# Two-scale attention and a gated FFN: attention on small array tiles, with x kept transposed on the chip

## The chip, the core and the metric

The kernel runs on one core of a Trainium2 chip. A core has five engines with instruction streams of their own: PE (TensorE, matmuls and weight loads), DVE (VectorE), ACT (ScalarE), POOL (GpSimd) and SP (SyncE, which here only issues transfers). Matmuls read SBUF and write PSUM. Sixteen DMA engines move data between DRAM and SBUF. The metric is the device time of one execution in microseconds (us), the median of several runs.

## The reference

```python
def _attn_ref(q, k, v):                       # each 8 x 8 x 576 x 64, float32
    factor = 4; Sd = S // factor; scale = 1.0 / np.sqrt(D)
    def sm_attn(qq, kk, vv):
        s = scale * np.matmul(qq, kk.transpose(0, 1, 3, 2))
        s = s - np.max(s, axis=-1, keepdims=True)
        a = np.exp(s)
        a = a / (np.sum(a, axis=-1, keepdims=True) + 1e-09)
        return np.matmul(a, vv)
    q_d = q.reshape(B, H, Sd, factor, D).mean(axis=3)      # k_d, v_d likewise
    out_up = np.repeat(sm_attn(q_d, k_d, v_d), factor, axis=2)
    mask = np.abs(pos[:, None] - pos[None, :]) < factor    # 7 keys for each query
    scores = np.where(mask, scale * np.matmul(q, k.transpose(0, 1, 3, 2)), -1e9)
    ...                                                    # softmax of the band
    return out_up + np.matmul(attn, v)

def _moe_ref(x, w_gate, w_val, w_out):        # x: 4608 tokens x 512
    gate = np.maximum(x @ w_gate, 0.0)        # 512 x 1536
    return gate * (x @ w_val) @ w_out         # 1536 x 512
```

x is the attention's output with the eight heads side by side. So each head has a coarse attention (144 x 144, over means of four rows), repeated four times, and a local one in which a query sees seven keys.

## The kernel before

**Pairs and chunks.** The 64 heads are taken as 32 pairs (hp); a pair's two heads lie on partitions 0-63 and 64-127 of the transposed tiles. The FFN takes 512 tokens at a time: nine chunks, each of 12 h tasks and 4 y tasks. An h task is 8 matmuls of 512 columns (4 for the gate at L170, 4 for the value at L175), a relu on ACT (L180) and a product on DVE (L182). A y task is 12 matmuls of 512 columns (L191) and a copy (L195). All matmul operands are float16.

**Loads.** `emit_load` issues q and k (L261) and two windows of v (L292) for a pair on SP's queue, 96 or 128 partitions with pieces of 64 floats, two pairs ahead. Weights come on ACT's queue as float32 (L140) and are cast there (L145).

**Attention of a pair.** `emit_mid` casts q on ACT (L301, L302), k and v on DVE (L303, L304, L307). `emit_mid_b` turns q and k on PE with an identity (L319, 12 matmuls), copies them out (L328 ACT, L330 DVE) and sums groups of four rows on DVE (L336, L342). `emit_compute` makes the coarse scores (L366), means of v (L377), the local scores in blocks of 96 queries by 128 keys (L405), exponentials without a maximum subtracted (L389, L415), a multiplication by a 0/1 band (L418), coarse output (L429), local output with a column of ones for the sum (L463), the coarse output repeated by a matmul (L475), and the normalised sum into `x_b` (L486, L492).

**x.** `x_b` goes to DRAM (L503) and comes back turned by transposing DMAs (L153), 512 tokens by 128 features at a time.

**Order.** The tile framework keeps the program's order on each engine and adds the waits. Two lists per pair (`sched`) put FFN tasks between its parts, 16 tasks over four pairs, the first in the second half of pair 5; tasks that don't fit run after the last pair (`tail`). Attention and FFN share eight PSUM buffers of one bank.

Of the kernel before, what the change touches and what calls it, by code (L numbers as in the profile page):

```python
# [14 lines left out]
DEBUG_MODE = "full"  # L15


def _np_constants():
    i = np.arange(128)[:, None]
    p = np.arange(96)[None, :]  # L20
    band = ((i - p >= 0) & (i - p <= 6)).astype(np.float16)
    m_first = band * (i >= 3)
    m_last = band * (i <= 98)
    masks = np.stack([m_first, band, band, band, band, m_last], axis=1)
    P72 = np.zeros((128, 3, 72), np.float16)
    rw = np.arange(3, 99)
    for sig in range(3):
        P72[rw, sig, 24 * sig + (rw - 3) // 4] = 0.25
    E72 = np.zeros((128, 3, 96), np.float16)
    t = np.arange(72)  # L30
    qq = np.arange(96)
    for a in range(3):
        E72[:72, a, :] = t[:, None] == (24 * a + qq[None, :] // 4)
    I96 = np.zeros((96, 128), np.float16)
    I96[:, :96] = np.eye(96)
    return masks, P72, E72, I96
# [17 lines left out]
def kernel(  # L54
# [12 lines left out]
    NH = B * H  # L67
    NP = NH // 2
    NQ = 96
    NB = S // NQ  # L70
    SD = S // 4
    KPAD = 16
    KW = KPAD + S + 32
    scale = float(1.0 / np.sqrt(D))
    D_MODEL = H * D
    D_FF = moe_w_gate.shape[1]
# [3 lines left out]
    NJJ = D_FF // 128  # L80

    masks_np, P72_np, E72_np, I96_np = _np_constants()
    masks_dr = nc.inline_tensor(masks_np, name="band_masks").ap()
    P72_dr = nc.inline_tensor(P72_np, name="p72").ap()
    E72_dr = nc.inline_tensor(E72_np, name="e_up").ap()
    I96_dr = nc.inline_tensor(I96_np, name="i96").ap()

    cpool = ctx.enter_context(tc.tile_pool(name="consts", bufs=1))
    masks_sb = cpool.tile([128, 6, 96], FP16, name="masks_sb")
    P72_sb = cpool.tile([128, 3, 72], FP16, name="p72_sb")  # L90
    E_sb = cpool.tile([128, 3, 96], FP16, name="E_sb")
    I96_sb = cpool.tile([96, 128], FP16, name="I96_sb")
    nc.sync.dma_start(masks_sb, masks_dr)
    nc.sync.dma_start(P72_sb, P72_dr)
    nc.sync.dma_start(E_sb, E72_dr)
    nc.sync.dma_start(I96_sb, I96_dr)

    drpool = ctx.enter_context(tc.tile_pool(name="scratch", bufs=1, space=bass.MemoryType.DRAM))
    x_dr = drpool.tile([NTOK, D_MODEL], FP16, name="x_dr")
    probe_dr = nc.dram_tensor("probe", (3, 128, KW), mybir.dt.float16, kind="Internal").ap() if DEBUG_MODE == "probe" else None  # L100

    wpool = ctx.enter_context(tc.tile_pool(name="weights", bufs=1))
    wg_sb = wpool.tile([128, 4, D_FF], FP16, name="wg_sb")
    wv_sb = wpool.tile([128, 4, D_FF], FP16, name="wv_sb")
    wo_sb = wpool.tile([128, NJJ, D_MODEL], FP16, name="wo_sb")
    wstg = ctx.enter_context(tc.tile_pool(name="wstage", bufs=5))

    psum = ctx.enter_context(tc.tile_pool(name="psum", bufs=8, space=bass.MemoryType.PSUM))
    a_nat = ctx.enter_context(tc.tile_pool(name="a_nat", bufs=8))
    a_vst = ctx.enter_context(tc.tile_pool(name="a_vst", bufs=4))  # L110
    a_16 = ctx.enter_context(tc.tile_pool(name="a_16", bufs=3))
    a_T = ctx.enter_context(tc.tile_pool(name="a_T", bufs=4))
    a_dT = ctx.enter_context(tc.tile_pool(name="a_dT", bufs=4))
    a_vw = ctx.enter_context(tc.tile_pool(name="a_vw", bufs=4))
    a_e = ctx.enter_context(tc.tile_pool(name="a_e", bufs=8))
# [3 lines left out]
    a_sm = ctx.enter_context(tc.tile_pool(name="a_sm", bufs=8))
    a_t2 = ctx.enter_context(tc.tile_pool(name="a_t2", bufs=4))  # L120
    a_x = ctx.enter_context(tc.tile_pool(name="a_x", bufs=2))
    f_xT = ctx.enter_context(tc.tile_pool(name="f_xT", bufs=8))
    f_r = ctx.enter_context(tc.tile_pool(name="f_r", bufs=3))
    f_gT = ctx.enter_context(tc.tile_pool(name="f_gT", bufs=20))
    f_y = ctx.enter_context(tc.tile_pool(name="f_y", bufs=1))

    wtasks = []
    for kk in range(4):
        wtasks.append((moe_w_gate, kk, wg_sb, kk))
        wtasks.append((moe_w_val, kk, wv_sb, kk))  # L130
    for jj in range(NJJ):
        wtasks.append((moe_w_out, jj, wo_sb, jj))

    st_w = {}

    def emit_wdma(i):
        src, row, dst, slot = wtasks[i]
        ncol = src.shape[1]
        t = wstg.tile([128, ncol], FP32, name="wstage", tag="wstage")
        nc.scalar.dma_start(t, src[bass.ts(row, 128), :])  # L140
        st_w[i] = t

    def emit_wcast(i):
        src, row, dst, slot = wtasks[i]
        nc.scalar.copy(out=dst[:, slot, :], in_=st_w.pop(i))  # L145

    ffn_state = {}

    def ffn_xbar1(c, m):
        if c not in ffn_state:  # L150
            ffn_state[c] = {"xT": [None] * 4, "gts": [], "y_sb": None}
        t = f_xT.tile([128, TCH], FP16, name="xT", tag="xT")
        nc.sync.dma_start(  # L153
            out=t,
            in_=_dap(x_dr, c * TCH * D_MODEL + m * 128, [[D_MODEL, TCH], [1, 128]]),
            transpose=True,
        )
        ffn_state[c]["xT"][m] = t

    def ffn_xbars(c):  # L160
        for m in range(4):
            ffn_xbar1(c, m)

    def ffn_task_h(c, jj):
        st = ffn_state[c]
        xts = st["xT"]
        h1 = psum.tile([128, TCH], FP32, name="h1_ps", tag="bank")
        h2 = psum.tile([128, TCH], FP32, name="h2_ps", tag="bank")
        for kk in range(4):
            nc.tensor.matmul(  # L170
                out=h1, lhsT=wg_sb[:, kk, bass.ts(jj, 128)], rhs=xts[kk],
                start=(kk == 0), stop=(kk == 3),
            )
        for kk in range(4):
            nc.tensor.matmul(  # L175
                out=h2, lhsT=wv_sb[:, kk, bass.ts(jj, 128)], rhs=xts[kk],
                start=(kk == 0), stop=(kk == 3),
            )
        r1 = f_r.tile([128, TCH], FP16, name="r1", tag="r1")
        nc.scalar.activation(out=r1, in_=h1, func=AF.Relu)  # L180
        gt = f_gT.tile([128, TCH], FP16, name="gT", tag="gT")
        nc.vector.tensor_tensor(out=gt, in0=r1, in1=h2, op=ALU.mult)  # L182
        st["gts"].append(gt)

    def ffn_task_y(c, ty):
        st = ffn_state[c]
        if st["y_sb"] is None:
            st["y_sb"] = f_y.tile([128, 4, D_MODEL], FP32, name="y_sb", tag="y_sb")
        y_ps = psum.tile([128, D_MODEL], FP32, name="y_ps", tag="bank")
        for jj in range(NJJ):  # L190
            nc.tensor.matmul(  # L191
                out=y_ps, lhsT=st["gts"][jj][:, bass.ts(ty, 128)],
                rhs=wo_sb[:, jj, :], start=(jj == 0), stop=(jj == NJJ - 1),
            )
        nc.scalar.copy(out=st["y_sb"][:, ty, :], in_=y_ps)  # L195
        if c == NCH - 1:
            nc.scalar.dma_start(
                _dap(out, (c * TCH + ty * 128) * D_MODEL,
                     [[D_MODEL, 128], [1, D_MODEL]]),
                st["y_sb"][:, ty, :],  # L200
            )
            if ty == 3:
                ffn_state.pop(c)
        elif ty == 3:
            nc.scalar.dma_start(
                _dap(out, c * TCH * D_MODEL,
                     [[D_MODEL, 128], [128 * D_MODEL, 4], [1, D_MODEL]]),
                st["y_sb"],
            )
            ffn_state.pop(c)  # L210

    def emit_task(t):
        kind = t[0]
        if kind == "h":
            ffn_task_h(t[1], t[2])
        elif kind == "y":
            ffn_task_y(t[1], t[2])
        elif kind == "wd":
            emit_wdma(t[1])
        elif kind == "wc":  # L220
            emit_wcast(t[1])

# [292 lines left out]
    for i in pre_dmas:  # L515
        emit_wdma(i)
# [50 lines left out]
```

## Time and profile before

| | us |
|---|---|
| median of 3 runs | 441.1 (439.14 to 441.73) |
| span of the profiled execution | 440.1 |
| busy in it: PE, DVE, ACT, POOL | 397.4, 298.4, 211.4, 7.7 |
| first FFN matmul starts | 71.8 |
| last copy of y starts | 436.4 |

The span is the time from the first to the last instruction of one execution; what lies around it is not in the profile. A row of the profile's groups reads: line, engine, operation, out<-in, count, busy time, mean of one. "PEld" are weight loads, which overlap matmuls. A matmul's record contains its latency (0.2 us), so records of consecutive matmuls overlap, and their price is the distance of their starts. "SPq" is an instruction that issues a transfer: its time is that of the issue, not of the data.

The rows that the change replaces, from the groups of instructions by shape:

```profile
L415 ACT ACTIVATE e_sb<-sc_ps 128x288 f16<-128x288 f32 x128 | 42.0, 416 | 1.1 <-PE sc_ps L405 1.1
L418 DVE TENSOR_TENSOR e_sb<-e_sb,masks_sb 128x288 f16<-128x288 f16 x128 | 36.3, 301 | 4.9 <-ACT e_sb L415 4.9
...
L475 PE MATMUL f_ps<-odn,E_sb 72*96 72x64 f16 x384 | 25.6, 220 | 0.0
...
L342 DVE TENSOR_REDUCE k_dT<-kT 128x144 f16<-128x576 f16 x32 | 23.7, 740 | 0.0
...
L389 ACT ACTIVATE e_d<-sd_ps 72x288 f16<-72x288 f32 x64 | 22.5, 402 | 16.9 <-PE sd_ps L366 16.8
...
L307 DVE CAST vwin<-vst 128x768 f16<-128x768 f32 x32 | 17.7, 553 | 6.5 <-DMA vst<-in_v_dram 6.5
```

### The profile page before, as it was taken

How to read it: one execution, taken by the hardware profiler on the slowest of the kernel's cores; microseconds unless marked ns; L12 is line 12 of the kernel's file. 1: busy time of each engine (PE TensorE's matmuls, PEld its weight loads, DVE VectorE, ACT ScalarE, POOL GpSimd, SP SyncE). 2: the span in 40 equal slices, each digit the busy share in tenths (PEclk: the TensorE clock that was granted, in tenths of full speed). 3: DMA queues.
4: the chain of work that ended last, by engine and by line, in shares of the span. 5: the costliest groups of instructions: out<-in, count | busy, mean ns of one | idle time of the engine just before them, and what ended most of it. 6: DMA issues, size and time to landing. Idle time of an engine off the chain costs nothing.

```text
span 440.1 us, 9037 instructions
## 1 busy us (share of the span) xinstructions
PE 397.4 (90%) x3408; PEld 227.6 (52%) x3408; DVE 298.4 (68%) x812; ACT 211.4 (48%) x485; POOL 7.7 (2%) x100
## 2 busy tenths in 40 slices
PE   0037778999999999999999999999999999999996
PEld 0026675555555555555565556555655654444442
DVE  0229998998789878977997799779966860330430
ACT  2435876564565455545564556445633532332331
POOL 0000000000000000000000000000000000000000
PEclk9999999999999999999999999999999999999999
DMA  8799989457777787577775646321123112200202
GB/s 288 245 311 224 278 226 243 107 114 174 188 185 172 166 207 176 135 165 215 173 162 132 191 105 138 76 105 33 30 36 109 27 39 48 97 0 9 87 0 95
DMA packets 171730, 60.64 MB, mean 138 GB/s; under 512 B 164264, under 2 KB 164520, under 8 KB 171688
## 3 DMA queue, kind: packets, MB, share of 16 engines
q1 hardware_dynamic: 164008, 41.21, 42.5%
q10 hardware_dynamic: 7680, 18.88, 11.4%
q8 instruction: 26, 0.43, 0.4%
q14 instruction: 16, 0.13, 0.1%
HBM read 41.20 MB, written 14.16 MB: 126 GB/s over the span
## 4 chain that ended last, share of the span: by engine, by line
PE 82%; DMA 7%; DVE 6%; SPq 3%; issue 1%; ACT 1%; DVEq 0%
PE h_ps L170 21%; PE h_ps L175 21%; PE y_ps L191 19%; PE tp_ps L319 3%; PE f_ps L475 3%; PE od_ps L429 3%; PE u_ps L463 3%; DMA vst<-in_v_dram 3%; PE vd_ps L377 3%; PE sc_ps L405 2%; DMA nat<-in_k_dram 2%; SPq L292 2%; PE sd_ps L366 1%; DMA out_dram<-y_sb 1%; DMA masks_sb<-band_masks 1%; SPq L261 1%
## 5 line engine op out<-in xcount | busy, mean ns | idle before, releaser
L170 PE MATMUL h_ps<-xT,wg_sb 128*128 128x512 f16 x432 | 112.1, 382 | 0.0
L175 PE MATMUL h_ps<-xT,wv_sb 128*128 128x512 f16 x432 | 111.7, 381 | 0.0
L191 PE MATMUL y_ps<-wo_sb,gT 128*128 128x512 f16 x432 | 95.7, 379 | 0.0
L175 PEld LDWEIGHTS <-wv_sb 128*128 128x128 f16 x432 | 42.5, 98 | 51.6 <-issue 1.1
L191 PEld LDWEIGHTS <-gT 128*128 128x128 f16 x432 | 41.5, 98 | 48.2
L170 PEld LDWEIGHTS <-wg_sb 128*128 128x128 f16 x432 | 40.3, 99 | 42.3 <-issue 1.6
L195 ACT COPY y_sb<-y_ps 128x512 f32<-128x512 f32 x36 | 21.1, 586 | 78.8 <-PE y_ps L191 72.8
L415 ACT ACTIVATE e_sb<-sc_ps 128x288 f16<-128x288 f32 x128 | 42.0, 416 | 1.1 <-PE sc_ps L405 1.1
L418 DVE TENSOR_TENSOR e_sb<-e_sb,masks_sb 128x288 f16<-128x288 f16 x128 | 36.3, 301 | 4.9 <-ACT e_sb L415 4.9
L463 PEld LDWEIGHTS <-e_sb 128*96 128x96 f16 x384 | 24.8, 138 | 12.0 <-DVE e_sb L418 6.5
L463 PE MATMUL u_ps<-vwin,e_sb 128*96 128x65 f16 x384 | 25.3, 220 | 6.2 <-DVE e_sb L418 6.2
L389 ACT ACTIVATE e_d<-sd_ps 72x288 f16<-72x288 f32 x64 | 22.5, 402 | 16.9 <-PE sd_ps L366 16.8
L394 DVE CAST vd_sb<-vd_ps 72x130 f16<-72x130 f32 x64 | 15.6, 284 | 20.4 <-PE vd_ps L377 20.4
L330 DVE CAST kT<-tp_ps 128x288 f16<-128x288 f32 x64 | 26.7, 442 | 1.5 <-PE tp_ps L319 1.5
L475 PE MATMUL f_ps<-odn,E_sb 72*96 72x64 f16 x384 | 25.6, 220 | 0.0
L429 PE MATMUL od_ps<-vd_sb,e_d 72*72 72x65 f16 x256 | 18.4, 206 | 7.8 <-DVE vd_sb L394 5.9
L328 ACT CAST qT<-tp_ps 128x288 f16<-128x288 f32 x64 | 23.5, 431 | 0.8 <-PE tp_ps L319 0.5
L342 DVE TENSOR_REDUCE k_dT<-kT 128x144 f16<-128x576 f16 x32 | 23.7, 740 | 0.0
L336 DVE TENSOR_REDUCE q_dT<-qT 128x144 f16<-128x576 f16 x32 | 23.6, 739 | 0.0
L475 PEld LDWEIGHTS <-E_sb 72*96 72x96 f16 x384 | 22.8, 138 | 0.0
L307 DVE CAST vwin<-vst 128x768 f16<-128x768 f32 x32 | 17.7, 553 | 6.5 <-DMA vst<-in_v_dram 6.5
L429 PEld LDWEIGHTS <-e_d 72*72 72x72 f16 x256 | 16.9, 123 | 10.0 <-issue 3.8
(556 smaller groups left out, 452.9 us busy)
## 6 DMA issues: line engine op xcount, KB each, us to landing
vst<-in_v_dram SPq DMA_DIRECT2D x62, 192.0 KB
nat<-in_q_dram SPq DMA_DIRECT2D x32, 288.0 KB
nat<-in_k_dram SPq DMA_DIRECT2D x32, 288.0 KB
out_dram<-y_sb ACTq DMA_DIRECT2D x8, 1024.0 KB
x_dr<-x_b SPq DMA_DIRECT2D x32, 144.0 KB
wstage<-in_moe_w_gate_dram ACTq DMA_DIRECT2D x4, 768.0 KB
wstage<-in_moe_w_val_dram ACTq DMA_DIRECT2D x4, 768.0 KB
wstage<-in_moe_w_out_dram ACTq DMA_DIRECT2D x12, 256.0 KB
```

The costliest lines, as they stand in the source:

```text
L170: nc.tensor.matmul(out=h1, lhsT=wg_sb[:, kk, bass.ts(jj, 128)], rhs=xts[kk], start=(kk == 0), stop=(kk == 3),)
L175: nc.tensor.matmul(out=h2, lhsT=wv_sb[:, kk, bass.ts(jj, 128)], rhs=xts[kk], start=(kk == 0), stop=(kk == 3),)
L191: nc.tensor.matmul(out=y_ps, lhsT=st["gts"][jj][:, bass.ts(ty, 128)], rhs=wo_sb[:, jj, :], start=(jj == 0), stop=(jj == NJJ - 1),)
L328: nc.scalar.copy(out=o, in_=tp)
L330: nc.vector.tensor_copy(out=o, in_=tp)
L336: nc.vector.tensor_reduce(out=q_dT, in_=qT[:, KPAD : KPAD + S].rearrange("p (t f) -> p t f", f=4), axis=mybir.AxisListType.X, op=ALU.add,)
L342: nc.vector.tensor_reduce(out=k_dT, in_=kT[:, KPAD : KPAD + S].rearrange("p (t f) -> p t f", f=4), axis=mybir.AxisListType.X, op=ALU.add,)
L415: nc.scalar.activation(out=esb, in_=scps[hh][:, :, 0:NQ], func=AF.Exp, scale=scale)
L418: nc.vector.tensor_tensor(out=esb, in0=esb, in1=masks_sb[:, 3 * g2 : 3 * g2 + 3, :], op=ALU.mult,)
L429: nc.tensor.matmul(out=od_ps[0:72, hh, tcx, :], lhsT=ed_sb[hh][:, c, bass.ts(tcx, 72)], rhs=vd_sb[hh][:, c, :], start=(c == 0), stop=(c == 1),
L463: nc.tensor.matmul(out=up[:, j, :], lhsT=e_sb[hh][j // 3][:, j % 3, :], rhs=vw[:, hh, j, :], start=True, stop=True,)
L475: nc.tensor.matmul(out=fp[:, j, :], lhsT=E_sb[0:72, j % 3, :], rhs=odn_sb[hh][0:72, j // 3, :], start=True, stop=True,)
```

## The change

Nearly the whole kernel is rewritten. What it does now:

- **x stays in SBUF, transposed** (`xT`, 128 x 4 x 4608 float16). `sums` makes the attention's output features by tokens, so the DRAM copy and its transposing DMAs are gone.
- **Local attention in blocks of 24 queries and 32 keys.** `scores` issues 48 matmuls of 64 x 32 by 32 columns on eight tiles of the array; `sums` 48 of 32 x 64 by 24 columns on eight tiles. The band is added as 0 or -1e9, and rows are normalised before `sums`.
- **Exact maxima** for both scales (`maxima`), subtracted before the exponentials: on POOL for the local rows (`dd`), as the bias of four ACT instructions for the coarse ones. Normalising is on POOL too (`weigh`); local weights are turned 32 by 32 on DVE (`turn_p`), coarse ones by a transposing DMA (`adT`).
- **q and k** are turned on PE for pairs 0 to 5 (`turn_pe`, which also sums groups of four by matmul), and by two transposing DMAs for the others (`turn_dma`, with the sums on POOL in `pool_qk`).
- **Weights** come by DMAs on POOL's queue that cast on the way; no cast on ACT.
- **One PSUM buffer `at` of four banks** for the attention, and four one-bank buffers for the FFN.
- **The order is written by hand.** Slots 0 to 3 carry no FFN work. In slot s the scores of pair s and the sums of pair s-1 stand between FFN units: 3, 3, 2, 2, 2 units in slots 4 to 8, four in the others (two before the sums, two after), and 36 units at the end.

```diff
-    x_dr = drpool.tile([NTOK, D_MODEL], FP16, name="x_dr")
-    psum = ctx.enter_context(tc.tile_pool(name="psum", bufs=8, space=bass.MemoryType.PSUM))
+    xT = pool.tile([128, 4, NTOK], FP16, name="xT")
+    fpsum = ctx.enter_context(tc.tile_pool(name="fps", bufs=4, space=bass.MemoryType.PSUM))
+    at = psum.tile([128, 4, 512], FP32, name="at")
...
+    def load_w(src, dst, lo, hi):
+        nc.gpsimd.dma_start(
+            dst[:, :, lo:hi], src.rearrange("(a p) f -> p a f", p=128)[:, :, lo:hi]
+        )
...
+    def turn_dma(p):
+        nc.sync.dma_start(
+            qT[p % 3][:, 0:S].rearrange("p (j t) -> p j t", j=6),
+            q16[p % 2].rearrange("p j f -> p (j f)"),
+            transpose=True,
+        )
...
+    def pool_qk(p):
+        qg = qT[p % 3][:, 0:S].rearrange("p (g f) -> p g f", f=4)
+        nc.gpsimd.tensor_tensor(out=ptq, in0=qg[:, :, 0:2], in1=qg[:, :, 2:4], op=ALU.add)
+        nc.gpsimd.tensor_tensor(
+            out=pd[p % 3][:, 0, :], in0=ptq[:, :, 0], in1=ptq[:, :, 1], op=ALU.add
+        )
...
+    def scores(p):
...
+                out=at[32 * x : 32 * x + 32, kc, 288:416],
+                lhsT=p32,
+                rhs=vt[:, :, m, :],
...
+                    out=at[0:72, h, 144 * c : 144 * c + 144],
+                    lhsT=pdt[lo : lo + 64, 0, 72 * c : 72 * c + 72],
+                    rhs=pdt[lo : lo + 64, 1, :],
...
+        for n in range(6):
+            for g in range(4):
+                c, m = n // 3, 4 * (n % 3) + g
+                for h in range(2):
+                    lo = 64 * h
+                    nc.tensor.matmul(
+                        out=at[32 * g : 32 * g + 32, 2 + h, 32 * n : 32 * n + 32],
+                        lhsT=qt[lo : lo + 64, 96 * n + 24 * g : 96 * n + 24 * g + 32],
+                        rhs=kt[lo : lo + 64, c, :, 6 * m : 6 * m + 8].rearrange("p r g -> p g r"),
+                        start=True,
+                        stop=True,
+                        tile_position=(lo, 32 * g),
+                    )
...
+    def maxima(p):
+        c = col[p % 2]
+        nc.vector.tensor_tensor(
+            out=sm[p % 2].rearrange("p (h n) j -> p h (n j)", h=2),
+            in0=at[:, 2:4, 0:192],
+            in1=_sap(mask, (0, 128), 0, [[0, 2], [1, 192]]),
+            op=ALU.add,
+        )
...
+        nc.vector.tensor_reduce(out=c[:, 0:12], in_=sm[p % 2], axis=AX.X, op=ALU.max)
+        nc.gpsimd.tensor_tensor(
+            out=dd[p % 2],
+            in0=sm[p % 2],
+            in1=_sap(c, (0, 128), 0, [[1, 12], [0, 32]]),
+            op=ALU.subtract,
+        )
...
+    def exps(p):
...
+        nc.scalar.activation(out=ee[p % 2], in_=dd[p % 2], func=AF.Exp, scale=scale)
+        nc.scalar.copy(out=vd16[p % 2], in_=at[:, 0:2, 288:416])
...
+    def weigh(p):
...
+        nc.gpsimd.tensor_tensor(
+            out=pp[p % 2],
+            in0=ee[p % 2],
+            in1=_sap(c, (0, 128), 24, [[1, 12], [0, 32]]),
+            op=ALU.mult,
+        )
...
+    def sums(p):
+        vt, w, vd, ad = vw[p % 4], pT[p % 2], vd16[p % 2], adT[p % 2]
+        for n in range(6):
+            for h in range(2):
+                for g in range(4):
                     nc.tensor.matmul(
+                        out=at[64 * h : 64 * h + 64, g, 24 * n : 24 * n + 24],
+                        lhsT=vt[32 * g : 32 * g + 32, h, n, :],
+                        rhs=w[32 * g : 32 * g + 32, 6 * h + n, 0:24],
...
+        nc.scalar.copy(
+            out=odx[p % 2].rearrange("p (g n m) -> p g n m", g=4, n=6),
...
+        nc.vector.tensor_tensor(
+            out=xT[:, kk, b * S : (b + 1) * S].rearrange(
...
+    for s in range(4, NP + 1):
+        a = per_slot.get(s, (1, 1, 1, 1))
...
+        if s + 3 < NP and s > 3:
+            load(s + 3)
+        if s < NP:
+            if s + 1 < NP and s + 1 >= N_PE:
+                pool_qk(s + 1)
+            if s + 2 < NP:
+                cast_q(s + 2, "act")
+            scores(s)
+            maxima(s)
+        ffn(a[0])
+        if s + 1 < N_PE:
+            turn_pe(s + 1)
+        if s < NP:
+            exps(s)
+            if s + 2 < NP:
+                cast_v(s + 2, "dve")
+            weigh(s)
+        ffn(a[1])
+        if s > 4:
+            sums(s - 1)
+        if s + 2 < NP:
+            cast_k(s + 2, 0, "act")
+            cast_k(s + 2, 1, "act")
+            turn_dma(s + 2)
+        ffn(a[2])
+        if s < NP:
+            turn_p(s)
+        ffn(a[3])
+    ffn(len(units) - pos[0])
```

More of the change, by code (lines that the diff above doesn't have):

```diff
@@ L14 @@
 ALU = mybir.AluOpType
-DEBUG_MODE = "full"
+AX = mybir.AxisListType
+N_PE = 6
+NEG = -1.0e9
 def _np_constants():
[L19 to L36, printed above, removed]
+    p = np.arange(128)
+    g, i = p // 32, p % 32
+    j = np.arange(32)
+    diff = (j[None, :] - 4) - i[:, None]
+    inside = np.abs(diff) <= 3
+    mask = np.zeros((128, 6, 32), np.float32)
+    for n in range(6):
+        key = 24 * (4 * n + g)[:, None] - 4 + j[None, :]
+        ok = inside & (key >= 0) & (key < 576)
+        mask[:, n, :] = np.where(ok, 0.0, NEG)
+    mask[i >= 24] = 0.0
+    p32 = np.zeros((128, 32), np.float16)
+    own = (i >= 4) & (i < 28)
+    p32[p[own], (6 * g + (i - 4) // 4)[own]] = 0.25
+    eye = np.zeros((96, 192), np.float16)
+    eye[:, :96] = np.eye(96)
+    eye[1:73, 96:168] = np.eye(72)
+    eye[np.arange(96), 168 + np.arange(96) // 4] = 1.0
+    return mask, p32, eye
 def _dap(t_ap: bass.AP, extra_off: int, dims) -> bass.AP:
@@ L119 @@
[L119 to L155, printed above, removed]
+    NJ = DF // 128
@@ new lines, in many @@
+    def many(n, shape, dt, name):
+        return [pool.tile(shape, dt, name=f"{name}{i}") for i in range(n)]
+    wg = pool.tile([128, 4, DF], FP16, name="wg")
+    wv = pool.tile([128, 4, DF], FP16, name="wv")
+    wo = pool.tile([128, NJ, DM], FP16, name="wo")
+    qst = many(3, [96, 2, 6, 64], FP32, "qst")
+    kst = many(3, [80, 2, 2, 256], FP32, "kst")
+    vst = many(3, [128, 2, 6, 64], FP32, "vst")
+    y_sb = many(4, [128, DM], FP32, "y_sb")
+    q16 = many(2, [96, 6, 128], FP16, "q16")
@@ L156, in ffn_xbar1 @@
+    def turn_dma(p):
+        nc.sync.dma_start(
+            qT[p % 3][:, 0:S].rearrange("p (j t) -> p j t", j=6),
+            q16[p % 2].rearrange("p j f -> p (j f)"),
             transpose=True,
         )
[L158 to L172, printed above, removed]
-            )
[L174 to L210, printed above, removed]
@@ L310, in emit_mid_b @@
[L310 to L318 removed]
+        nc.sync.dma_start(
+            kT[p % 3].rearrange("p c r g -> p (c r) g"),
+            k16[p % 2].rearrange("p c r f -> p (c r f)"),
+            transpose=True,
+        )
@@ new lines, in exps @@
+    def exps(p):
+        c = col[p % 2]
+        for h in range(2):
+            for cc in range(2):
+                hc = 2 * h + cc
+                nc.scalar.activation(
+                    out=e_d[p % 2][0:72, h, cc, 0:6, 0:24],
+                    in_=at[0:72, h, 144 * cc : 144 * cc + 144].rearrange("p (n j) -> p n j", j=24),
+                    func=AF.Exp,
+                    bias=c[0:72, 40 + hc : 41 + hc],
+                    scale=scale / 16.0,
+                    accum_out=c[0:72, 44 + hc : 45 + hc],
+                )
+        nc.scalar.activation(out=ee[p % 2], in_=dd[p % 2], func=AF.Exp, scale=scale)
+        nc.scalar.copy(out=vd16[p % 2], in_=at[:, 0:2, 288:416])
@@ L425, in emit_compute @@
-        od_ps = psum.tile([72, 2, 2, 65], FP32, name="od_ps", tag="bank")
-        for hh in (0, 1):
-            for tcx in range(2):
-                for c in range(2):
-                    nc.tensor.matmul(
-                        out=od_ps[0:72, hh, tcx, :],
-                        lhsT=ed_sb[hh][:, c, bass.ts(tcx, 72)],
-                        rhs=vd_sb[hh][:, c, :],
-                        start=(c == 0),
-                        stop=(c == 1),
-                    )
-        odn_sb = [None, None]
@@ new lines, with unit_h @@
+    n_h = [0]
+    n_y = [0]
+    def unit_h(c, j):
+        h1 = fpsum.tile([128, TCH], FP32, name="h1_ps", tag="f")
+        h2 = fpsum.tile([128, TCH], FP32, name="h2_ps", tag="f")
+        for ps, w in ((h1, wg), (h2, wv)):
+            for kk in range(4):
+                nc.tensor.matmul(
+                    out=ps,
+                    lhsT=w[:, kk, 128 * j : 128 * j + 128],
+                    rhs=xT[:, kk, TCH * c : TCH * c + TCH],
+                    start=(kk == 0),
+                    stop=(kk == 3),
+                )
+        r = r1[n_h[0] % 3]
+        n_h[0] += 1
+        nc.scalar.activation(out=r, in_=h1, func=AF.Relu)
+        nc.vector.tensor_tensor(out=gT[c % 2][:, j, :], in0=r, in1=h2, op=ALU.mult)
@@ new lines, in unit_y @@
+    def unit_y(c, t):
+        ps = fpsum.tile([128, DM], FP32, name="y_ps", tag="f")
+        for j in range(NJ):
+            nc.tensor.matmul(
+                out=ps,
+                lhsT=gT[c % 2][:, j, 128 * t : 128 * t + 128],
+                rhs=wo[:, j, :],
+                start=(j == 0),
+                stop=(j == NJ - 1),
+            )
+        y = y_sb[n_y[0] % 4]
+        n_y[0] += 1
+        nc.scalar.copy(out=y, in_=ps)
+        nc.sync.dma_start(
+            _dap(out, (c * TCH + t * 128) * DM, [[DM, 128], [1, DM]]), y
+        )
@@ new lines, with ffn @@
+    units = []
+    for c in range(NCH):
+        for j in range(NJ):
+            units.append(("h", c, j))
+            if c and j % 3 == 1:
+                units.append(("y", c - 1, j // 3))
+    units += [("y", NCH - 1, t) for t in range(4)]
+    pos = [0]
+    def ffn(n):
+        for _ in range(n):
+            kind, c, j = units[pos[0]]
+            pos[0] += 1
+            (unit_h if kind == "h" else unit_y)(c, j)
+    nc.sync.dma_start(eye, eye_dr)
+    for t in kst[0], vst[0]:
+        nc.gpsimd.memset(t, 0.0)
@@ new lines, with cast_early @@
+    load(0)
+    nc.scalar.dma_start(p32, p32_dr)
+    nc.scalar.dma_start(mask, mask_dr)
+    for t in k16 + e_d:
+        nc.vector.memset(t, 0.0)
+    load(1)
+    load(2)
+    for t in qT:
+        nc.gpsimd.memset(t[:, S:], 0.0)
+    def cast_early(p):
+        cast_q(p, "act")
+        cast_k(p, 0, "dve")
+        cast_k(p, 1, "dve")
+        cast_v(p, "pool")
+    cast_early(0)
+    turn_pe(0)
+    w_at = {1: [0], 2: [1], 3: [2, 3]}
+    for s in range(4):
+        cast_early(s + 1)
+        scores(s)
[3 more added lines that the diff above has]
+        weigh(s)
+        for i in w_at.get(s, ()):
+            load_w(moe_w_gate, wg, 384 * i, 384 * i + 384)
+            load_w(moe_w_val, wv, 384 * i, 384 * i + 384)
+        load(s + 3)
+        turn_p(s)
+        if s:
+            sums(s - 1)
@@ new lines @@
+    sums(3)
+    load_wo(0, 4)
+    load_wo(4, 8)
+    load_wo(8, 12)
+    per_slot = {4: (1, 1, 1, 0), 5: (1, 1, 1, 0), 6: (1, 1, 0, 0), 7: (1, 1, 0, 0), 8: (1, 1, 0, 0)}
+    for s in range(4, NP + 1):
+        a = per_slot.get(s, (1, 1, 1, 1))
+        if s == 4:
+            cast_q(5, "act")
+            cast_k(5, 0, "act")
+            cast_k(5, 1, "act")
+            cast_v(5, "dve")
+        if s + 3 < NP and s > 3:
+            load(s + 3)
+        if s < NP:
[3 more added lines that the diff above has]
+                cast_q(s + 2, "act")
+            scores(s)
+            maxima(s)
+        ffn(a[0])
+        if s + 1 < N_PE:
+            turn_pe(s + 1)
+        if s < NP:
+            exps(s)
+            if s + 2 < NP:
+                cast_v(s + 2, "dve")
+            weigh(s)
+        ffn(a[1])
+        if s > 4:
+            sums(s - 1)
+        if s + 2 < NP:
[4 more added lines that the diff above has]
+        if s < NP:
+            turn_p(s)
+        ffn(a[3])
```

514 lines of the change are left out of this document (193 added, 321 removed).

## The prediction

> **What bounds the kernel now.** I read the page's engine rows first, then its forty slices, then the chain that ended last.
>
> ```profile
> PE 397.4 (90%) x3408; PEld 227.6 (52%) x3408; DVE 298.4 (68%) x812; ACT 211.4 (48%) x485; POOL 7.7 (2%) x100
> ...
> PE   0037778999999999999999999999999999999996
> ...
> DMA  8799989457777787577775646321123112200202
> ...
> PE 82%; DMA 7%; DVE 6%; SPq 3%; issue 1%; ACT 1%; DVEq 0%
> ```
>
> There are two regimes. For six slices (66 us) PE is not full while the DMA engines are; then PE is full to the end. The windows of one stretch of each, 10 to 70 us and four pairs of the steady part (columns: length, busy time and instructions of PE, PEld, DVE, ACT, POOL, granted clock, DMA share, GB/s):
>
> ```profile
> 10.00:70.00 60.00, 32.50 (x386) 28.54 (x387) 41.07 (x128) 37.09 (x79) 1.07 (x15) 1.00 0.96 252
> ...
> 148.87:192.59 43.72, 43.65 (x409) 24.97 (x408) 36.82 (x103) 22.63 (x56) 1.22 (x15) 1.00 0.74 174
> ```
>
> In the steady part four pairs take 43.72 us, 10.93 each, and PE has no gap. The chain's y rows have 24 matmuls of 512 columns in 5.18 us, 0.2158 each (0.42 ns a column). Four pairs carry 144 such, 31.1 us; the remaining 12.6 are attention, 3.16 us of PE a pair. All 1296 FFN matmuls take 279.7 us. The first one starts at 71.97, the last matmul ends at 436.3, and copy, store and end take 3.8: 72 + 279.7 + 26.5 pairs x 3.16 + 3.8 = 439, against the span of 440.1. So the time is: start of the FFN, plus a fixed 280, plus PE time of attention, plus PE's waits. The x round trip through DRAM, which the change removes, is worth nothing by itself: PE waits for no xT.
>
> How PE spends a pair's attention is in the timeline (start, duration, line, matmuls):
>
> ```profile
> 219.54 0.32 PE L366 MATMUL sd_ps<-q_dT,k_dT 64*72 64x144 f16 x4
> 219.79 0.54 PE L377 MATMUL vd_ps<-vwin,p_sb 128*72 128x130 f16 x6
> 220.26 0.43 PE L405 MATMUL sc_ps<-qT,kT 64*128 64x96 f16 x12
> 220.71 0.49 PE L429 MATMUL od_ps<-vd_sb,e_d 72*72 72x65 f16 x8
> 221.04 0.68 PE L319 MATMUL tp_ps<-I_sb,qk_3835 96*128 96x96 f16 x12
> 221.55 0.38 PE L170 MATMUL h_ps<-xT,wg_sb 128*128 128x512 f16 x1
> ```
>
> Two things matter. Where the shape of the array changes (64 rows to 128 and back) starts leave about 0.09 us unexplained by columns: the last sc of 96 columns starts at 220.49 and streams to 220.53, the next weight load starts at 220.62. And the sc matmuls, alternating between partitions 0-63 and 64-127, start in twos 3 ns apart, a new two every 40 ns (96 columns): 20 ns each. Full-height ones take 32 (od, 65 columns) to 57 (vd, 130).
>
> **The change, part by part.**
>
> Slots 9 to 31 (23 of them): two h units, sums, a y and an h, 36 FFN matmuls, 7.77 us. Attention on PE: vd 8 matmuls in four column tiles, two rounds of 128 columns, 0.17; sd 4, 0.16 as now; 48 of 32 columns in eight tiles; 48 of 24 columns in eight tiles; od 4 of 144 columns in two tiles, 0.15. No row shows matmuls of 24 or 32 columns. Their price lies between 3 ns (the distance in a two) and 32 (the od period). I take 10, half of sc's 20, since eight tiles instead of two can be in flight but each needs its own weight load: 0.48 for each 48. Seven changes of shape at 0.09, and a first exposed weight load of 0.05 to 0.09 at each, make 0.96. X = 0.17 + 0.16 + 0.48 + 0.48 + 0.15 + 0.96 = 2.4 us against 3.16. The transposes (12 at 41 ns, 0.5) leave PE.
>
> A new wait on PE: `at` is one buffer, so sums(s-1) wait until scores(s) have been read, in the built program until the vd16 copy on ACT, which stands behind the exponentials there. From the scores' last start: 0.24 to DVE's start; add of 384 from PSUM 0.54 (L486); maxima of 576, 0.66 (L342's 0.74, consecutive ones start 0.08 early); scale 0.12 (L438); maxima of 384, 0.48: 2.04. Then dd on POOL. The trace has only memsets there; bounds are 0.54 (the DVE row) and 1.6 (three times it); I take 1.0, about double, because POOL's memsets of 12 to 32 elements (0.12 to 0.15) are no quicker than small DVE work. Then ee 0.49 and vd16 0.36 on ACT (between L389's 0.40 for 288 and L195's 0.59 for 512) and four hand-overs of 0.08: 4.2 us. Cover: two h units, 3.45, plus 0.18 of switching. PE waits 0.6 in every slot; behind it are the sums, the y, the h and the next scores. A slot takes 7.77 + 2.4 + 0.65 = 10.8; 23 take 249.
>
> The rest lies beside PE. Per slot: DVE 2.0 for maxima, three gates at 0.68, v's cast 0.55 (L307), sums and reciprocals of weigh 0.9, the 32-wise turn about 0.5, the add of 576 about 0.75: 6.7 us. ACT: q cast 1.0 (two of L301's 0.5), four exps at 0.4, ee and vd16 0.85, k casts 1.2, three relus and y at 0.6, odx 0.35: 7.4. POOL: seven operations with 2208 elements, 5.8 at 1.0 for 384. SP: six loads at about 0.6, three transposes at 1.13, a store at 0.35: 7.4. DMA: 4544 packets of 256 bytes at 18 ns (42.5% of 16 engines' span for 164008) over 16 engines, 5.1, plus k and y: 6.7. All are under 10.8; the nearest would be the bound if PE got under 7.5. The removed work (masks L418, the reduces L336 and L342, L328 and L330, x_b) was beside PE too and gives nothing.
>
> ```profile
> L153 SPq DMA_TRANSPOSE xT<-x_dr x36: 1122/1134/2708, 60.9 to 367.0; - x36
> ```
>
> The turned q and k land, by the same queue's transposes, 2.4 to 5.0 us after issue (most 2.6). POOL's pool_qk(s+1) stands before dd(s) and waits for them; the circle sums, odx 0.45, k casts 1.2, landing 2.6, two k adds 1.1, dd 1.0, ee and vd16 0.9, sums 0.8 is 8.1 us, under the slot.
>
> Start. q's first cast is at 9.45 now, k's at 12.79, v's at 21.34, behind 3 MB of weights on ACT's queue. Weights now go later through POOL, so pair 0 (1 MB at about 290 GB/s) is there by 8 to 9; a v cast on POOL (0.55 to 1.6) puts scores(0) at 10.5. Slots 0 to 3 have no FFN and are a chain: scores at the slow early rate (tp 279 ns early, 205 later) 2.0; to vd16 5.0, as two ACT copies of turn_pe come first; sums 1.3; the add behind turn_p, 1.1: 9.4, less in slot 0 (7.5) and more in slot 3 (two sums, 11.7): 38. With 1.5 for weight DMAs on POOL the FFN's slot 4 begins at 50, 22 us earlier than now, though slots 4 to 8 carry only 12 h units. Their two or three units hide inside the chain: scores 1.3, to vd16 4.2, sums 0.9, odx and the add before the next scores 1.4, so 7.8; the circle gives 8.1. Slot 4 has turn_pe in place of sums, 7.8; slot 5 a third unit, 8.5; for 6 to 8, while DMA still brings weights, I take 9.5. Together 45. Weight pieces have 16 us or more before use: nothing. Tail: 372 FFN matmuls 80.3, sums(31) 1, copy, store and end 4: 85.3.
>
> Sum: 50 + 45 + 249 + 85.3 = 429 of span; the median of the runs is 1.0 above the profiled span: 430.
>
> **Rivals.**
>
> *Tiles fully side by side, chain covered.* For: twos 3 ns apart. Against: only two tiles were ever seen. At that distance a group of 48 takes 0.2 and X is 1.8; with dd at DVE's 0.54 the wait is 0.1: slots 9.7, 223; 41 and 47 before, 85 after: 397. [...]
>
> *A floor per small matmul: slower.* For: no row shows fewer than 20 ns on average, and od's 65 columns take 32. Against: the twos. At 30 ns X is 2.4 + 96 x 0.020 = 4.3; slots 12.75, 293; 54 and 54 before, 86 after: 488. It decides from 13.6 ns: 11 us of gain over 32 x 96 matmuls is 3.6 ns each above my 10. [...]
>
> *POOL and the circle.* For: POOL, idle 98%, becomes a link of the chain. dd at 1.6 adds 0.6 to each wait: 14 + 5 in slots 4 to 8 + 8 before: 457. If the turns land at 5.0 too the circle is 12.2 and the slots take 1.4 more: 473. [...]
>
> **Chances.** Mine 0.42, side by side 0.15, floor 0.22, POOL 0.21. Of mine, a spread of 415 to 445, about 0.3 lies more than 1% (4.4 us, what the runs' 439.1 to 441.7 can tell) below 441.1: faster 0.46, same 0.12, slower 0.42. The range leaves out half of the first rival and of the floor: 402 to 472; mine alone 415 to 445.
>
> **What would show it.** In the profile after: the first h near 52 us; 48 scores in about 0.5 us; slots of 10.8; POOL's dd near 1.0; PE waiting 0.6 a slot for ACT's vd16 before the sums; the transposes' landing 2.6. I am wrong if small matmuls are above 14 ns, if a POOL row is over 1.6, or if PE waits first for turned q or k.

## The result, and the profile after

| | before | after |
|---|---|---|
| median, us | 441.4 (439.14 to 442.4) | 592.2 (589.94 to 594.27) |
| ratio | | 1.341, 95% interval 1.336 to 1.346 |
| span of the profiled execution | 440.1 | 592.3 |
| granted clock, mean | 1.000 | 0.881 |

The change made the kernel 34% slower; 430 had been forecast. The page of the changed kernel:

```profile
PE 405.7 (68%) x5048; PEld 190.9 (32%) x5048; DVE 223.4 (38%) x443; ACT 222.7 (38%) x595; POOL 164.1 (28%) x225
...
PE   0232213736657786787787887787777859999997
...
PEclk9999999767677979878878788888887779999999
DMA  2449999465665767766666666666767241100002
...
PE 32%; SPq 20%; DMA 19%; issue 11%; POOL 10%; ACT 4%; DVE 3%; POOLq 0%; ACTq 0%; DVEq 0%
PE y_ps L449 15%; PE h_ps L434 13%; SPq L171 11%; DMA kT<-k 9%; DMA kst<-in_k_dram 9%; SPq L374 3%; POOL dd L336 3%; POOL ptk L265 3%; POOL pd L268 2%; SPq L140 2%; SPq L145 2%; PE at L391 2%; ACT e_d L348 2%; SPq L247 1%; ACT vd L357 1%
```

No engine is full before slice 34, where attention is over. The DMA engines are not full either behind slice 7, mostly at 50 to 80%. Yet the chain spends 39% of the span in transfers and their issue, above all the loads of k and v and the turned k. A mean of 65% over sixteen engines, and transfers on the chain all the same: that pair of lines asks how the work lies on the sixteen.

The starts of the scores in the trace give the time by stage (slots 9 to 30 are 22):

| us | scores(4) at | slots 4 to 8 | slots 9 to 30 | scores(31) to the end | span |
|---|---|---|---|---|---|
| forecast | 50 | 45 | 238 (10.8 each) | 96 | 429 |
| changed kernel | 100.4 | 70.8 | 326.8 (14.9) | 94.3 | 592.3 |

Everything that has loads beside it is late; what has none took what was forecast. SP's own rows, over one slot of the steady part (start, duration, line, transfer):

```profile
293.69 0.42 SPq L136 DMA_DIRECT2D qst<-in_q_dram  x1
294.16 0.58 SPq L140 DMA_DIRECT2D kst<-in_k_dram  x1
294.84 7.93 SPq L171 DMA_DIRECT2D vst<-in_v_dram  x4
302.88 2.44 SPq L374 DMA_TRANSPOSE adT<-e_d  x1
305.37 1.28 SPq L247 DMA_TRANSPOSE qT<-q  x1
306.75 1.23 SPq L252 DMA_TRANSPOSE kT<-k  x1
308.07 0.52 SPq L459 DMA_DIRECT2D out_dram<-y_sb  x1
308.64 0.42 SPq L136 DMA_DIRECT2D qst<-in_q_dram  x1
```

SP never rests: 14.95 us from one load of q to the next, 7.9 of them in issuing four v loads that move less than q and k together. The same slot on POOL, ACT and PE:

```profile
308.19 0.67 POOL L260 TENSOR_TENSOR ptq<-qT 128x288 f32<-128x288 f16 x1 [8.97 <-DMA qT<-q]
...
311.00 0.83 POOL L336 TENSOR_TENSOR dd<-sm,col 128x384 f32<-128x384 f32 x1
...
311.87 0.52 ACT L356 ACTIVATE ee<-dd 128x384 f16<-128x384 f32 x1 [2.00 <-POOL dd L336]
...
312.70 0.54 PE L391 MATMUL at<-pT,vw 32*64 32x24 f16 x48 [2.35 <-ACT vd L357]
...
313.41 4.42 PE L449 MATMUL y_ps<-wo,gT 128*128 128x512 f16 x12
```

POOL waits 8.97 us for the turned q, whose issue stood behind the v loads; dd stands behind that on POOL, ee behind dd, the copy vd16 behind ee, and PE's sums behind the copy. Most of the twelve matmuls of y start 0.43 us apart, against 0.2158 before: the granted clock is 0.86 in the four slots from 306 to 365 us.

Why the v loads block is in the reports on the semaphores, sixteen for q and for each v load, three for k (from the trace, us after the issue; the others of a line follow within its last two numbers):

```
                                        first    ...                 last
q  of pair 0, 96 partitions             3.1 ...                      4.0
k  issued at 164.58, 74 partitions      0.6                          9.8, 9.9
v  issued at 165.15, 32 partitions      14 of them at 5.0 to 5.4,    9.7, 9.8
v  issued at 168.60, 32 partitions      14 at 2.4 to 3.2,            6.6, 6.8
```

Of k's reports one comes at once and two late. Of the sixteen of each of these v loads, fourteen come together and two some 4 us behind, 174.8 to 175.4, just after k's (174.3 and 174.5). The reading: two engines have k's 296 packets of 1 KB and their sixteenth of all else. The trace does not name a packet's engine, so this rests on the reports, and on the runs below.

The theory (A): the time is set by the two engines that hold k, and SP, which issues in order, is blocked behind them (the profile shows how long an issue took, not what it waited for). Rivals: (B) four v loads of 32 partitions cost SP 2 us each by themselves; (C) POOL's order, pool_qk(s+1) ahead of dd(s), is what makes late turns costly.

### The profile page after: what moved, and what is told of

The parts are those of the page before. It is cut to its first block, busy times and chain, and to the rows that moved or that the text cites. A ratio compares the mean times of both kernels' runs of the same rounds, so it can differ in the third digit from the quotient of the medians.

```text
span 592.3 us, 12326 instructions
## 1 busy us (share of the span) xinstructions
PE 405.7 (68%) x5048; PEld 190.9 (32%) x5048; DVE 223.4 (38%) x443; ACT 222.7 (38%) x595; POOL 164.1 (28%) x225
## 4 chain that ended last, share of the span: by engine, by line
PE 32%; SPq 20%; DMA 19%; issue 11%; POOL 10%; ACT 4%; DVE 3%; POOLq 0%; ACTq 0%; DVEq 0%
PE y_ps L449 15%; PE h_ps L434 13%; SPq L171 11%; DMA kT<-k 9%; DMA kst<-in_k_dram 9%; SPq L374 3%; POOL dd L336 3%; POOL ptk L265 3%; POOL pd L268 2%; SPq L140 2%; SPq L145 2%; PE at L391 2%; ACT e_d L348 2%; SPq L247 1%; ACT vd L357 1%
## 5 line engine op out<-in xcount | busy, mean ns | idle before, releaser
L444 DVE TENSOR_TENSOR gT<-r,h_ps 128x512 f16<-128x512 f16 x108 | 74.0, 686 | 165.7 <-PE h_ps L434 158.3
L449 PE MATMUL y_ps<-wo,gT 128*128 128x512 f16 x432 | 134.5, 478 | 0.0
L434 PE MATMUL h_ps<-xT,wg 128*128 128x512 f16 x432 | 118.5, 399 | 0.0
L434 PE MATMUL h_ps<-xT,wv 128*128 128x512 f16 x432 | 114.2, 388 | 0.0
L391 PE MATMUL at<-pT,vw 32*64 32x24 f16 x1536 | 18.2, 199 | 112.9 <-ACT vd L357 111.0
L443 ACT ACTIVATE r<-h_ps 128x512 f16<-128x512 f32 x108 | 64.6, 598 | 74.4 <-PE h_ps L434 74.0
L449 PEld LDWEIGHTS <-gT 128*128 128x128 f16 x432 | 48.7, 117 | 73.6 <-issue 46.0
L434 PEld LDWEIGHTS <-wv 128*128 128x128 f16 x432 | 43.4, 101 | 54.7 <-issue 6.5
L434 PEld LDWEIGHTS <-wg 128*128 128x128 f16 x432 | 41.7, 102 | 51.5 <-issue 10.5
L391 PEld LDWEIGHTS <-vw 32*64 32x64 f16 x1536 | 18.2, 122 | 124.3 <-issue 113.8
L356 ACT ACTIVATE ee<-dd 128x384 f16<-128x384 f32 x32 | 16.7, 523 | 91.4 <-POOL dd L336 91.4
L348 ACT ACTIVATE e_d<-at,col 72x144 f16<-72x144 f32 x128 | 46.6, 371 | 3.7 <-DVE col L331 3.5
L365 POOL TENSOR_TENSOR e_d<-e_d,col 72x576 f16<-72x576 f16 x32 | 36.6, 1143 | 13.7 <-issue 11.1
L192 ACT CAST k<-kst 74x512 f16<-74x512 f32 x54 | 30.7, 618 | 0.8 <-DMA kst<-in_k_dram 0.8
```

Of the source, the lines that this page charges most:

```text
L192: nc.scalar.copy(out=out, in_=in_)
L348: nc.scalar.activation(out=e_d[p % 2][0:72, h, cc, 0:6, 0:24], in_=at[0:72, h, 144 * cc : 144 * cc + 144].rearrange("p (n j) -> p n j", j=24),
L365: nc.gpsimd.tensor_tensor(out=ed, in0=ed, in1=_sap(c, (0, 72), 48, [[1, 4], [0, 6], [0, 24]]), op=ALU.mult)
L391: nc.tensor.matmul(out=at[64 * h : 64 * h + 64, g, 24 * n : 24 * n + 24], lhsT=vt[32 * g : 32 * g + 32, h, n, :], rhs=w[32 * g : 32 * g + ...
L434: nc.tensor.matmul(out=ps, lhsT=w[:, kk, 128 * j : 128 * j + 128], rhs=xT[:, kk, TCH * c : TCH * c + TCH], start=(kk == 0), stop=(kk == 3),)
L443: nc.scalar.activation(out=r, in_=h1, func=AF.Relu)
```

## The experiments

Where k's load is edited, lines stand one below those of the changed kernel, or of the kernel before (L306 is L305). Where no interval is given there is one run, and before's median on the same chip was 441.1 to 441.9.

### k on sixteen engines

```
-        lo, hi = (1 if p == 0 else 0), (73 if p == NP - 1 else 74)
-        nc.sync.dma_start(st[lo:hi], ...)
+        for lo, hi in ((1, 65), (65, 74)) if p == 0 else ((0, 64), (64, 73)) if p == NP - 1 else ((0, 80),):
+            nc.sync.dma_start(st[lo:hi], ...)
```

> The changed kernel, but k's load covers 80 partitions in pairs 1 to 30 (the rows behind 73 are read and not used), and 64 and 9 in pairs 0 and 31, in place of 74 and 73. Theory A (k's 296 packets of 1 KB lie on two DMA engines, which carry them in about 8 us a slot beside their sixteenth of the rest, about 6.6, so that every DMA's last part comes late): first k landing within 5 us, one v DMA issued in under 1 us, slots of 10.8 to 11.5, granted clock near 1.00, 425 to 455 us. Rival B (the four v DMAs of 32 partitions cost SP some 2 us each by themselves): SP stays full, slots stay near 15, over 570. Rival C (POOL's pool_qk ahead of dd, waiting for turned q and k that land in 2.5 to 4.7): slots of 13 or more, over 510.

Measured: 441.9 us, ratio to before 1.0007 (0.998 to 1.004). k's sixteen reports now come together, for the load in the rows below 4.3 to 5.3 us after its issue. SP in a steady slot, and the page:

```profile
263.28 0.43 SPq L136 DMA_DIRECT2D qst<-in_q_dram  x1
263.76 0.72 SPq L141 DMA_DIRECT2D kst<-in_k_dram  x1
264.58 1.96 SPq L172 DMA_DIRECT2D vst<-in_v_dram  x4
```
```profile
PE   2543049587789999989999999998989999999996
...
PEclk9999996788899999999999999999999999999999
DMA  8999999999989999999999999999854211010102
...
PE 50%; ACT 11%; DMA 9%; DVE 9%; POOL 7%; issue 7%; SPq 5%; DVEq 0%; POOLq 0%; ACTq 0%
```

The same four v loads issue in 1.96 us, so B is out. 150 us go with the partition counts of one load, and more bytes are moved for it (320 KB a pair instead of 296). The granted clock returns with it: 0.973, with nothing done about it.

### Only the inner pairs

Pairs 0 and 31 keep their 73 partitions:

```
+        for lo, hi in ((lo, hi),) if p in (0, NP - 1) else ((0, 80),):
```

> As the first, but pairs 0 and 31 keep their 73 partitions. Theory A: pair 0's k still lands about 34 us after its issue and scores(0) starts 10 to 12 us later than in the first, the steady slots are as there: 10 to 15 us above it. Rivals B and C: within 10 us of the changed kernel's 592.

Measured: 461.8 us. scores(0) is at 22.1 against 11.0 in the run before, as A said. The expectation put k's landing too high: the trace has pair 0's k 16.7 us after the issue, not 34; the later reports that had been counted belong to the next use of that semaphore. The end lost as well, since slots 28 and 29 take 12.1 and 20.7 (10.0 and 11.5 in the run before) while pair 31's k comes through one engine: 20 us in all for two pairs of 32.

### k on one engine

```
+        for lo, hi in ((lo, hi),) if p in (0, NP - 1) else ((0, 73), (73, 74)):
```

> The changed kernel with k's load in pairs 1 to 30 as 73 partitions and one, so that 292 of its packets lie on one DMA engine. Theory A: this engine needs about 15 + 6.6 us a slot, slots of 21 to 24, 760 to 850 us. Rivals B and C: one more DMA on SP at about 0.6 a slot, 592 to 615.

Measured: 745.9 us. Four slots of it (length, then busy time and instructions of PE, PEld, DVE, ACT, POOL, granted clock, DMA share, GB/s):

```profile
404.50:482.60 78.10, 48.16 (x600) 21.49 (x599) 26.01 (x53) 26.16 (x73) 20.11 (x28) 0.76 0.44 90
```

B and C are far off; A is right in kind and somewhat high. k lands 15.5 us after the issue. The mean slot from 9 to 29 is 19.8 us here, 15.1 with two engines, 10.4 with sixteen. The trace's 1 KB packets (150 to 300 us) took 49.3 ns on the mean here and 54.5 with two: if the engine never rests, 292 of them are 14.4 us and leave 5.4 for the rest, 148 are 8.1 and leave 7.0. The rest had been taken at 6.6 for both; why it is less with one engine is not shown. The sixteen engines are busy 0.44 on the mean in that row, and PE's clock and its waits are at their worst.

### The kernel before, with k on two engines

Its k load of 96 partitions is cut into 74 and 22, nothing else:

```
+                for lo, hi in ((0, 74), (74, 96)) if src is k else ((0, 96),):
+                    nc.sync.dma_start(nt[lo:hi], ...)
```

> The kernel before, with each pair's k load of 96 partitions cut into 74 and 22. Theory A: 888 packets of 256 bytes on two engines at 18 ns, 8 us a pair beside about 6 of the rest, so 14 a pair against 10.9: the last k comes near 32 x 14 = 450 and 80 us of FFN follow, 490 to 540. Rivals B and C (nothing is wrong with such a load by itself): one more DMA on SP, 439 to 446.

Measured: 496.1 us. The page and the waits:

```profile
PE   0024544669999999799999998999999699999996
...
PE 61%; SPq 21%; DMA 12%; DVE 2%; issue 2%; ACT 1%; DVEq 0%
```
```profile
DVE qk L304 <- DMA nat<-in_k_dram: 64.0, 14, 19.7
```

A kernel that has no matmuls of 24 or 32 columns, no POOL link and no q turned by DMA loses 54 us by such a load. The slow load alone is enough to cost time.

### Weights later

With k on sixteen engines 442 is still 12 over the forecast. By stage: scores(4) at 59.8, slots 4 to 8 56.7, slots 9 to 30 229.5 (10.4 each), the end 94.7. The loss is before slot 9; from 36 to 75 us loads and weights together have a DMA share of 1.24 to 1.38. So wo's loads were put into slots 5 to 7.

```
-    load_wo(0, 4); load_wo(4, 8); load_wo(8, 12)
+        if s in (5, 6, 7):
+            load_wo(4 * s - 20, 4 * s - 16)
```

A second kernel also moves the last of four pieces of wg and wv from slot 3 to slot 4:

```
-    w_at = {1: [0], 2: [1], 3: [2, 3]}
+    w_at = {1: [0], 2: [1], 3: [2]}
...
+        if s == 4:
+            load_w(moe_w_gate, wg, 1152, 1536)
+            load_w(moe_w_val, wv, 1152, 1536)
```

> k on 16 engines, and the three loads of wo (1 MB each) issued in slots 5, 6 and 7 instead of behind slot 3. Theory D (what k on 16 engines still has over the forecast lies in slots 3 to 8, where weights and pair loads have the DMA engines over-full, share 1.2 to 1.4, so that adT(3) lands 11 us late and v of pair 6 about 8): scores(4) near 50 instead of 59.8, scores(9) at 100 to 108 instead of 116.5, slots from there on 10.0 as before it, 424 to 433 us. Rival E (the bytes only move: pair loads of slots 5 to 8 now wait for wo, or the first y for wo): 437 to 445.

> As wo_later, and the last of four pieces of wg and wv issued in slot 4 instead of slot 3. D: another 0 to 5 us less than wo_later. Rival: unit h 9 of slot 7 waits for its piece, 0 to 8 us more.

Measured: 446.6 us, ratio 1.013 (1.010 to 1.016), and 448.4, 1.018 (1.012 to 1.024). The expectation of a gain fell. With wo later scores(4) came 2.0 us earlier, and slots 4 to 8 took 4.9 longer (1.6 and 8.8 in the second kernel). Slots 5 to 8 have a wait of 4.5 to 5.3 before the sums (wo later, slots 6 and 7, with POOL's rows of slot 7):

```profile
90.01 0.59 PE L392 MATMUL at<-pT,vw 32*64 32x24 f16 x48 [5.33 <-ACT vd L358]
...
99.36 0.65 POOL L261 TENSOR_TENSOR ptq<-qT 128x288 f32<-128x288 f16 x1 [7.09 <-DMA qT<-q]
...
101.73 0.83 POOL L337 TENSOR_TENSOR dd<-sm,col 128x384 f32<-128x384 f32 x1
...
103.43 0.55 PE L392 MATMUL at<-pT,vw 32*64 32x24 f16 x48 [4.65 <-ACT vd L358]
```

It is the changed kernel's chain again: the turned q comes late, now beside wo, and dd stands behind it. That is rival C, in the place where it has a price.

### The two orders: POOL and ACT

Both on the kernel with wo later. One moves pool_qk(s+1) behind dd(s):

```
-            if s + 1 < NP and s + 1 >= N_PE: pool_qk(s + 1)
             ...
             scores(s)
             maxima(s)
+            if s + 1 < NP and s + 1 >= N_PE: pool_qk(s + 1)
```

> As wo_later, with pool_qk(s+1) behind dd(s) on POOL, so that dd no longer waits for turned q and k. Rival C's price in this state: if dd waits for them in the steady slots, up to 0.5 a slot, 5 to 12 us less than wo_later; if q and k are there in time, within 2 us of it.

The other moves the copy vd16 ahead of ee on ACT, so that the last reader of the scores no longer waits for dd:

```
+        nc.scalar.copy(out=vd16[p % 2], in_=at[:, 0:2, 288:416])
         nc.scalar.activation(out=ee[p % 2], in_=dd[p % 2], func=AF.Exp, scale=scale)
-        nc.scalar.copy(out=vd16[p % 2], in_=at[:, 0:2, 288:416])
```

> As wo_later, with the copy vd16 ahead of ee on ACT, so that sums(s-1) wait for the last reader of the scores and no longer for POOL's dd and ee. If that wait is on the chain in the steady slots (0.3 to 0.5 of each 10.0): 8 to 12 us less than wo_later. If the DMA engines (share about 1.0) already set the 10.0: within 2 us of it.

Measured: 430.7 us (ratio 0.976, 0.972 to 0.980) and 436.1 (0.990, 0.985 to 0.995), against 446.6: 16 and 10.5 us, in the first above what was expected. The first took it from slots 4 to 8 (61.6 to 50.4) and from the hiccups later: slots 9 to 30 went from 230.8, with slots of up to 13.1, to 221.7, all of 10.0 to 10.1 but one of 11.4. The second took its 10 us from slots 9 to 30 alone (220.9). Slots 4 to 8 took 63.3: PE no longer waits there for vd16, but 21.8 us for the add into xT, which stands behind the sum of ee on DVE, and so still behind dd.

### The order alone, and the parts together

Four more: the changed kernel with POOL's order alone; k on sixteen with POOL's order and wo where the changed kernel has it; the same with vd16 ahead of ee; and that with pair 5's load behind the transpose adT(3) on SP:

```
-        load(s + 3)
+        for p in {0: (3,), 1: (4,), 3: (5, 6)}.get(s, ()):
+            load(p)
```

> The changed kernel with k still on two DMA engines, and only pool_qk(s+1) moved behind dd(s) on POOL. Theory A (the two engines set the slot, whatever POOL's order): slots stay at 14 to 15, 575 to 595 us. Rival C (the order is the main cause, late q and k only start it): slots of 12 or less, under 530.

> k on 16 engines, wo's loads where the changed kernel has them, pool_qk(s+1) behind dd(s). Theory C2 (with k mended, dd behind late turns is what is left in slots 4 to 9; wo_later's loss of 5 came through the same wait): slots 5 to 9 at 9 to 11, from there on an even 10.0, 424 to 432 us. If the gain of 16 needed the later wo: 436 to 442.

> As k16_pool, with vd16 ahead of ee on ACT. If PE's remaining wait before the sums (about 0.2 to 0.3 a slot) is on the chain: slots of 9.7 to 9.8, 5 to 9 us less than k16_pool. If PE is full at 10.0: within 2 us.

> As k16_pool_vd, with the load of pair 5 moved from slot 2 to slot 3, behind the transpose adT(3) on SP. If adT(3)'s landing (11 us late, PE waits for it before slot 4) is held by pair 5's packets ahead of it: scores(4) at 48 to 54 instead of about 60, 3 to 8 us less. If pair 5 is then late for slot 4: 0 to 6 us more.

| | us | ratio to before | scores(4) at | slots 4 to 8 | slots 9 to 30 |
|---|---|---|---|---|---|
| POOL's order, k on two engines | 578.3 | one run | 95.6 | 67.9 | 318.4 |
| k on 16, POOL's order | 429.1 | 0.972 (0.969 to 0.975) | 61.4 | 49.1 | 221.9 |
| and vd16 first | 420.9 | 0.955 (0.948 to 0.961) | 60.9 | 48.7 | 215.2 |
| and pair 5 later | 423.6 | 0.959 (0.956 to 0.963) | 48.4 | 61.8 | 216.9 |

With k on two engines the order is worth 14 us of 150; the wait only changes its name, from POOL's dd to the turned weights of the dilated half:

```profile
PE at L401 <- DMA adT<-e_d: 86.0, 25, 17.8
```

With k on sixteen it is worth 13 (441.9 to 429.1), and where wo is issued no longer matters (429.1 and 430.7): the loss by "wo later" had come through dd. So C holds as a second cause, not as the first. POOL's wait for the turned q falls from 102.5 us to 6.4.

The third row is faster than both kernels. Five of its steady slots, 9.70 us each:

```profile
256.90:305.40 48.50, 48.50 (x747) 23.37 (x744) 32.56 (x66) 32.41 (x91) 26.10 (x35) 1.00 1.08 183
```

PE is full. 36 FFN matmuls at 0.2158 are 7.77, so attention takes 1.93 us of PE a pair, against 3.16 in the kernel before. The last row shows why slot 4 is late: with pair 5's packets behind it, adT(3) lands in time and scores(4) starts 12 us earlier, as expected; then pair 5 is late and slot 4 takes 28.9. The wait changed its place, and the total did not fall. What would shorten that stage was not found.

## Why the prediction was wrong

**The step that failed** is "DMA: 4544 packets of 256 bytes at 18 ns ... over 16 engines, 5.1, plus k and y: 6.7", with "SP: six loads at about 0.6", and the sentence that all this lies beside PE. It divided by sixteen what, by the reports, lay on two. By that reading the runs showed in its place, by slot, 8.1 us of k's packets on each of two engines (148 at 54.5 ns) beside 7.0 of the rest, 15.1 together, and 7.9 us of SP in four v loads that take 1.96 with k's load on 80 partitions. In the kernel before, the steady loads of q, k and v have 96 or 128 partitions and report sixteen times, but its trace has an early row of the other kind: pair 0's first v load of 125 partitions, on that kernel's chain, with one report at 2.4 us and five at 9.9 to 10.4.

```profile
5.32 10.42 DMA vst<-in_v_dram
```

The partition counts of the new loads, 74 and 73, stand in the changed kernel (L139). Why the partition count matters is not shown; the loads that ran show this much. After a first report (0.6, 0.7 and 2.4 us) the load of 74 partitions has two late reports (9.8 and 9.9), that of 73 one (15.5, in the kernel with k on one engine) and that of 125 five (9.9 to 10.4); those of 96 and 80 have sixteen together (3.1 to 4.0 and 4.3 to 5.3). The times agree with it: 592.2 us for the changed kernel with 74, 745.9 with 73 and one, 441.9 with 80, and 496.1 for the kernel before with 74 and 22. The prediction had not weighed that early row of the kernel before. With 148 packets of k on each of two engines a slot is near 15 us, not 10.8, and the forecast gain is a loss.

**By stage.** Slots 9 to 30: 10.8 forecast, 14.9 measured, 10.4 with k on sixteen engines. Of the 163 us between 429 and 592, 89 lie here, 50 before slot 4, 26 in slots 4 to 8, and -2 at the end.

**The terms of the slot.** X was 2.4 and is 1.93 in the slot where PE is full. "I take 10" for a small matmul: the starts are 7.9 ns apart for 32 columns and 7.3 for 24 (medians of the groups of pairs 9 to 30 in the changed kernel). That is 0.23 of the 0.47 by which X was too high; most of the rest lies in the seven changes of shape with exposed loads, taken at 0.96 (0.77 is left for them in one slot of the run with PE full, when each group's starts and its last matmul's columns are taken off). The wait of 0.6 before the sums: 0.5 a slot with k on sixteen, none with vd16 first. POOL's dd, taken at 1.0, is 0.84; bounds of 0.54 and 1.6 held it.

**The start.** "At about 290 GB/s" and "FFN's slot 4 begins at 50": with k mended the first 36 us move 174 GB/s and the FFN begins at 60.3. The rate came from early slices of the kernel before, in which its large weight transfers have a part. scores(0) still came at 11.0 (10.5 forecast); the time is lost in slots 0 to 3, where PE waits 11.1 us for adT(3). The mended kernel is 12 over the forecast: 10 here, 12 in slots 4 to 8 (of which POOL's order is 8), less 8 in the later slots and 1 at the end. That k on 16 with POOL's order comes to 429.1, next to the 430 forecast, is luck: 16 us too long before slot 9, 16 too short in slots 9 to 30.

**The rivals.** The floor did not come: at 7.9 ns nothing reaches 13.6. Nor did the 3 ns of the first rival. "POOL and the circle" named the right link, POOL behind the turned q, and priced it at 457 to 473 (its circle of 12.2 does not add up: 0.6 more for dd and 2.4 for the turns make 11.1 of the 8.1). Its causes, slow POOL rows and slow turns, were not the ones: in the slot shown the turned q was there 2.8 us after its issue, as forecast. The issue was late, behind the v loads on SP.

## What to carry to other kernels

Before costing a load by its bytes, look at its number of partitions and at its reports: here a load of 74 partitions had two late reports and one of 73 had one, those of 80 and 96 had sixteen together, and 80 in place of 74 took the kernel from 592.2 to 441.9 us. SP's queue, which issued in order, carried the delay to the transfers behind: four v loads took SP 7.93 us behind k's load of 74 partitions and 1.96 behind that of 80. In a profile the sign was a chain with 39% in transfers and their issue at a mean DMA share of 0.65 (306 to 365 us); reports of which most came together and two some 4 us late pointed to the load, and the runs confirmed it. And on an in-order engine, work for the next step that waits for a transfer belongs behind work of this step that others wait for (here 441.9 to 429.1 us).

## What was not expected of the hardware

256-byte packets cost more in the changed kernels than the 18 ns of the forecast: 28.5 ns on the mean with k on sixteen engines, 27.1 in the changed kernel, 18.2 in the kernel before (from the traces; the median is 18 in each). Full engines alone are not the reason, for between 10 and 70 us of the kernel before, at a DMA share of 0.96, the mean is 19.0. What makes them dearer stays open. Yet a DMA share of 1.08 in the fastest kernel does not set its slot: PE is full beside it.

After waits of 2 to 6 us on PE the granted clock fell to a half, in slots 9 to 30 for 3.4 or 6.8 us at a time, and matmuls of 512 columns started 0.43 us apart. Such a stretch of the changed kernel, behind the wait of 2.35 us shown above:

```profile
314.36:317.77 3.41, 3.41 (x10) 1.23 (x9) 0.72 (x2) 0.48 (x1) 0.00 (x0) 0.50 0.47 113
```

The shortest of these waits was 1.86 us (ending at 385.1, half the clock from 386.0), while one of 1.68 us (ending at 223.8) left it full until 235.8. How much of the 150 us the clock took by itself was not separated: no run had the waits without it. By its mean of 0.881 it is at most 0.119 of 592 us, 70 us (an estimate).
